# A searched schedule for a Sinkhorn attention and top-1 expert kernel

## Chip, core and metric

The kernel runs on one core of one Trainium2 chip, in a single launch. The metric is the device time of one execution in microseconds (us). The core has five engines that run side by side: TensorE (PE in the profile) multiplies matrices and writes to PSUM, a memory of eight banks; VectorE (DVE) and ScalarE (ACT) read PSUM and do the elementwise work; GpSimd (POOL) does elementwise work in SBUF, the core's main memory, and here issues the loads; SyncE (SP) issues the stores. An engine works off its instructions in the order in which the program emits them, so the order chosen at build time is what decides who waits.

## What is computed

Attention over blocks, with keys and values mixed between blocks by a matrix that five Sinkhorn rounds make from `sort_net`; then each of the 3072 tokens goes through one of eight experts, the one with the largest logit.

```python
batch, n_heads, seq, head_dim, n_blocks = 4, 8, 768, 64, 8        # float32 inputs

for _ in range(5):                                   # P = sort_net, one 8 x 8 matrix for each head
    P = P - np.max(P, axis=-1, keepdims=True)
    P = np.exp(P)
    P = P / (np.sum(P, axis=-1, keepdims=True) + 1e-09)
    P = P / (np.sum(P, axis=-2, keepdims=True) + 1e-09)
k_sorted = np.einsum('bhij,bhjcd->bhicd', P, k_b)    # v_sorted the same; k_b has 8 blocks of 96 rows
scores = scale * np.matmul(q_b, k_sb.transpose(0, 1, 2, 4, 3))      # each block with its mixed keys
attn = exp(scores - max) / (sum + 1e-09)
x = (attn @ v_sb)  as  [3072, 512]                   # heads side by side

logits = x @ w_gate                                  # [3072, 8]
expert_idx = np.argmax(logits, axis=1)
gate_w = softmax(logits)[chosen]
for e in range(8):
    h = np.maximum(x[mask] @ w1[e], 0.0)             # w1[e]: 512 x 1024
    out[mask] = gate_w[mask, None] * (h @ w2[e])     # w2[e]: 1024 x 512
```

## The kernel before

The four batches are worked off one after another, overlapped. For each batch the kernel guesses one expert from the mean of the values (a "vote"), loads that expert's weights only, and sends all the batch's tokens through it. Tokens that chose another expert get weight zero, and a general path at the end, behind an `If`, adds them; with this draw no token needs it, and its body isn't run.

The program is emitted by a planner that runs at build time. Every piece of work is a task with an engine (or a choice of two), a cost in us, the tasks that it comes after, and a priority. The planner simulates the engines, takes at each step the task that can start first (the lowest priority value among those within a short look ahead), and emits the instructions in this order. Where it foresees a gap on TensorE early on, it puts in idle matmuls.

```python
class Plan:
    LAG = {("pe", "act"): 0.3, ("pe", "dve"): 0.3, ("act", "pe"): 0.2, ...}
    FIRM, SWITCH, STAY = -900, 0.09, 20
    FETCH, QUIET = 6.0, (14.5, 17.0, 3.9)           # how soon TensorE's next 256 instructions are there

    def fill(self, t):
        at = self.free.get("pe", self.begin)
        while t.start < self.until and t.start - at > 0.25:
            n = 80 if at < self.warm else 512 if t.start - at > 0.5 else 128
            ...                                      # one idle matmul of n columns into a free bank
```

GpSimd issues the loads, which turn float32 into bfloat16 on the way. Their order is fixed by a chain:

```python
    def load_w1(ev, i, piece):                       # a quarter of the columns of all rows
        at = slice(piece * F // PIECES, (piece + 1) * F // PIECES)
        nc.gpsimd.dma_start(out=w1s[i][:, :, at], in_=w1_r[bass.ds(ev, 1), :, :, at].rearrange("e p c f -> p (e c) f"))

    def load_w2(ev, i, piece):
        at = slice(piece * FC // PIECES, (piece + 1) * FC // PIECES)
        nc.gpsimd.dma_start(out=w2s[i][:, at], in_=w2_r[bass.ds(ev, 1), :, at].rearrange("e p c d -> p (e c) d"))

    for name in ("zero vr1", "zero ksT1", "ones vs1", "rev", "ones", "expand k", "expand v"):
        later[name].behind = w2_at[0][-1]
    for b in range(2, B):
        later[f"vote add{b}"].behind = w2_at[b - 1][-1]

    chain = [*FIRST_LOADS, *loads(0)[2:], *w1_at[0], *w2_at[0], *loads(1)]
    chain += [later[n] for n in ("expand k", "expand v", "zero ksT1")] + loads(2)
    for b in range(1, B):
        chain += [*w1_at[b], *w2_at[b], *(loads(3) if b == 1 else [])]
```

Values are first laid out anew ("relay", into `vr`), on VectorE or, for batch 0, also on ScalarE. The vote of batches 1 to 3 adds up the 48 rows of each partition on GpSimd, by halves:

```python
            def run_add(e):
                tt = nc.gpsimd.tensor_add
                n = HB // 2
                tt(v_tmp, vr[i2][:, :, :n], vr[i2][:, :, n:HB])
                while n > 3:
                    n //= 2
                    tt(v_tmp[:, :, :n], v_tmp[:, :, :n], v_tmp[:, :, n:2 * n])
                tt(v_tmp[:, :, 0], v_tmp[:, :, 0], v_tmp[:, :, 1])
                tt(v_sum[i2].rearrange("p (d t) -> p d t", t=2), v_tmp[:, :, 0], v_tmp[:, :, 2])
```

Then follow: q transposed and k mixed (three groups each, evacuated from PSUM by ACT or DVE), v mixed (four groups), and eight steps of scores, exponential, product with v, normalising, transposing and copying to `xT`. The operands `expand_k` and `expand_v`, made on GpSimd, spread the Sinkhorn matrices of batches 1 to 3 over the partitions (`rep`, lines 516 and 542). The gate of a batch ends in `gws`:

```python
            nc.vector.scalar_tensor_tensor(out=gws[:, b], in0=picks[:, b, :, 0], scalar=top[b][:, :1],
                                           in1=gates[:, b], op0=ALU.is_equal, op1=ALU.mult)
```

The expert takes a batch in two halves of 384 tokens; the first half of batch 0 goes in two parts of 192:

```python
            parts = 2 if b == half == 0 else 1
            n = NH // parts
            for r, fc in ((r, fc) for r in range(parts) for fc in range(FC)):
                t = add(f"h{b}.{half}.{fc}.{r}", {"pe": 0.66 / parts + 0.02 * (parts - 1)}, ... mm_hidden(
                            bank(pb)[:, :n], w1s[i2], xTs[b], lo, lo + n, fc),
                        [w1_at[b][fc * PIECES // FC], *turn_of[b][s0:s0 + steps], *(hT_user[hi] or [])], at, opens=pb, n=DC)
                relus[r].append(add(f"relu{b}.{half}.{fc}.{r}", ...))
```

Of the kernel before, what the change touches and what calls it, by code (L numbers as in the profile page):

```python
# [13 lines left out]
ALU = mybir.AluOpType  # L14
# [15 lines left out]
class Banks:  # L30


    def __init__(self, n, only=None):
        self.n, self.only, self.at = n, only, None


class Plan:
# [9 lines left out]
    FETCH, QUIET = 6.0, (14.5, 17.0, 3.9)  # L47
    BLOCK_AT, BLOCK, PACE, WAIT = 191, 256, 12.5, 300

    def __init__(self, dma_at=2.1, begin=1.4, warm=5.6, until=32.0):  # L50
        self.begin, self.warm, self.until = begin, warm, until
        self.tasks, self.free = [], {}
        self.bank = [0.0] * 8
        self.dma_free = dma_at
        self.order = []
        self.mode = "full"
        self.count, self.block, self.fetched = 0, self.BLOCK_AT + self.BLOCK, None

# [26 lines left out]
    def due(self):  # L85

        return self.fetched + (self.QUIET[2] if self.QUIET[0] < self.fetched < self.QUIET[1] else self.FETCH)
# [16 lines left out]
    def fill(self, t):  # L104

        at = self.free.get("pe", self.begin)
        while t.start < self.until and t.start - at > 0.25:
            n = 80 if at < self.warm else 512 if t.start - at > 0.5 else 128
# [28 lines left out]

    def schedule(self):
        waiting = {t: len(t.after) for t in self.tasks}
# [7 lines left out]
        open_ = [t for t in self.tasks if not waiting[t]]  # L147
        seq = {t: i for i, t in enumerate(self.tasks)}
        firm = [t for t in self.tasks if t.prio < self.FIRM]
        while open_:  # L150
            choice = None
            soon, due = {}, []
            for t in firm:
                if t.start is not None:
                    continue
                at = 0.0
                for a in t.after:
                    e = next(iter(t.cost))
# [6 lines left out]
                if at is not None:  # L165
                    soon[t] = at + min(t.cost.values())
                    if len(t.cost) == 1:
                        due.append((next(iter(t.cost)), at))
            per = {}
            for t in open_:  # L170
# [6 lines left out]
                opts = []  # L177
                for e, us in t.cost.items():
                    if e == "pe" and t.mode != self.mode:
                        us += self.SWITCH  # L180
                    s = max(self.free.get(e, 0.0), bank_at)
                    for a in t.after:
                        lag = 0.0 if a.lands is not None else self.LAG.get((a.engine, e), 0.15)
                        s = max(s, a.end + lag)
                    if t.prio >= self.FIRM:
                        for d, at in sorted(due, key=lambda x: x[1]):
                            if d == e and s < at + 0.3 and s + us > at + 0.08:
                                s = at + 0.31
                    if e == "pe":
                        s = self.fetch(t, s, us)  # L190
                    opts.append((s + us, s, e))
                end, s, e = min(opts)
# [17 lines left out]
            if t.lands is not None:  # L210
                if t.lands:
                    rate = 2.43 if self.dma_free < 13 else 2.85
                    self.dma_free = max(self.dma_free, end + 0.9) + t.lands * rate
                    t.end = self.dma_free + 1.6
                else:
# [6 lines left out]
            if t.closes is not None:  # L222
                for i in range(t.closes.n):
                    self.bank[t.closes.at + i] = t.end
            self.order.append(t)
            open_.remove(t)
            for n in then[t]:
                waiting[n] -= 1
                if not waiting[n]:
                    open_.append(n)  # L230
# [6 lines left out]
def kernel(  # L237
# [67 lines left out]
    xTs = [sb([P, DC, S], BF16, f"xT{i}") for i in range(B)]  # L305
# [3 lines left out]
    outs = [sb([P, MD], F32, f"o{i}") for i in range(4)]  # L309
# [26 lines left out]

    engines = {"act": nc.scalar, "dve": nc.vector, "pool": nc.gpsimd}
# [20 lines left out]
    def add_load_q(b, after=()):  # L358
        q_at[b] = [add(f"load q{b}", {"pool": 0.73}, lambda e: load_qk(q, q_in, b, 0, CS),
                       after=[*after, *q_done.get(b - 2, [])], prio=b, lands=1.5)] * 3  # L360

    def add_load_k(b, parts, after=()):
        n = CS // parts
        got = []
        for i in range(parts):
            got.append(add(f"load k{b}.{i}", {"pool": 0.73},
                           lambda e, i=i: load_qk(k, k_in, b, i * n, n),
                           after=[*after, *k_done.get(b - 2, [])], prio=b, lands=1.5 / parts))
        k_at[b] = [got[g * parts // 3] for g in range(3)]

    def add_load_v(b, after=()):
        def run(e):
            nc.gpsimd.dma_start(out=v_in[b % 2], in_=v[b].rearrange("h (x c) d -> (h x) c d", c=HB))
        v_at[b] = add(f"load v{b}", {"pool": 0.73}, run,
# [8 lines left out]
    def load_w1(ev, i, piece):  # L383
        at = slice(piece * F // PIECES, (piece + 1) * F // PIECES)
        nc.gpsimd.dma_start(out=w1s[i][:, :, at], in_=w1_r[bass.ds(ev, 1), :, :, at].rearrange("e p c f -> p (e c) f"))  # L385
# [31 lines left out]
    for i in range(2):  # L417
# [6 lines left out]
        pads["vr", i] = add(f"zero vr{i}", {"pool" if i else "dve": 0.96 if i else 0.5}, zero_vr, prio=5 if i else -940)  # L424
        pads["ksT", i] = add(f"zero ksT{i}", {"pool": 1.9}, zero_ksT, prio=5 if i else FIRST + 7)
# [7 lines left out]
    for i in range(2):  # L433
        pads["vs", i] = add(f"ones vs{i}", {"pool": 1.0}, lambda e, i=i: ones_vs(e, i),
# [49 lines left out]
    ek1 = add("expand k", {"pool": 1.2}, lambda e: run_expand(expand_k, NB * CQ), [mk_ident], prio=5)  # L484
    ev1 = add("expand v", {"pool": 0.8}, lambda e: run_expand(expand_v, NB * 2), [mk_ident], prio=5)
# [123 lines left out]
    SPAN, PREP, STEPS, STEP = 100, 4, 40, 6.5  # L609
    RELAY = {"act": 0.86, "dve": 0.49}  # L610

    def add_attention(b):
# [5 lines left out]
        for d0 in range(0, D // 2, cut):  # L618
# [8 lines left out]
            relays.append(add(f"relay{b}.{d0}", {"dve": 0.82} if b else RELAY, run_relay,  # L627
# [13 lines left out]
        else:  # L641
            def run_add(e):
                tt = nc.gpsimd.tensor_add
                n = HB // 2
                tt(v_tmp, vr[i2][:, :, :n], vr[i2][:, :, n:HB])  # L645
                while n > 3:
                    n //= 2
                    tt(v_tmp[:, :, :n], v_tmp[:, :, :n], v_tmp[:, :, n:2 * n])  # L648
# [35 lines left out]
        w1_at[b] = [add(f"load w1.{b}.{r}", {"pool": 0.75 if r else 1.9}, lambda e, r=r: run_w1(e, r),  # L684
                        [t4, *relu_of.get(b - 2, [])], A - 20 if b else -940, lands=2.0 / PIECES)
                    for r in range(PIECES)]
        w2_at[b] = [add(f"load w2.{b}.{r}", {"pool": 0.65}, lambda e, r=r: load_w2(val["ev"], i2, r),
                        outs_of.get(b - 2, []), A - 20, lands=2.0 / PIECES) for r in range(PIECES)]
        top_at[b] = add(f"top{b}", {"pool": 0.2}, lambda e: nc.gpsimd.tensor_scalar(
# [28 lines left out]
        for g in range(3):  # L718
# [16 lines left out]
            def run_ev(e, g=g, kb=kb):  # L735
# [343 lines left out]
```

## Time and profile before

| what | value |
|---|---|
| time, median of 3 | 162.43 us (161.91 to 163.8) |
| profiled execution | 162.2 us, span 160.5 us |
| hidden matmuls (line 879) | 288, busy 49.9 us |
| output matmuls (line 884) | 200, busy 45.8 us |
| idle matmuls (line 120) | 98, busy 9.9 us |
| read from HBM, written to it | 35.68 MB, 6.29 MB |

The profile's views that matter here: the busy share of each engine, whole and in 40 slices of the span; the waits (who waited for whom: total us, times, longest); the chain of work that ended last, followed back from the end, as start, length and what ran; and the timeline, all instructions in order of time with the idle time ahead of each. "L879" is line 879 of the kernel. PEld is the loading of weights into TensorE. A busy TensorE includes time in which matmuls only overlap in its pipeline, so the length of a chain piece divided by its matmuls tells more than the mean of one. PEclk is the clock that TensorE was granted, in tenths.

### The profile page before, as it was taken

The page shows a single profiled execution, that of the slowest core. Times are in us where ns is not written, and L with a number is a line of the kernel's source. Part 1 is how long each engine was busy: PE and PEld are TensorE (multiplying, and loading weights), DVE is VectorE, ACT ScalarE, POOL GpSimd, SP SyncE. Part 2 cuts the span into 40 slices and gives each one's busy share as a digit, 9 for nine tenths or more (in the row PEclk, how much of TensorE's full clock was granted, in tenths as well). Part 3 has the DMA queues.
Part 4 walks back from the last instruction along what each step waited for, and adds up shares of the span by engine and source line. Part 5 has one row for each costly group of instructions (what it writes and reads, how often), then busy time and mean ns, then how long its engine had stood idle before and what let it go on. Part 6 is the DMA issues. An engine that isn't in the chain of part 4 may idle for free.

```text
span 160.5 us, 5478 instructions
## 1 busy us (share of the span) xinstructions
PE 146.1 (91%) x2313; PEld 98.1 (61%) x2313; DVE 87.4 (54%) x220; ACT 97.2 (61%) x163; POOL 66.4 (41%) x110
## 2 busy tenths in 40 slices
PE   6989888699899999779999999999999999999950
PEld 6758767595656656537556666675566656545440
DVE  4885788669938928712946674383446734400010
ACT  3159897373777596624567867576578465637340
POOL 6940795996920968929379100950000000000000
PEclk9999999999999999987999999999999999999999
DMA  3999499999999999999999902799831023023051
GB/s 20 193 202 185 52 141 202 216 211 213 222 230 253 222 197 232 250 233 212 204 197 245 230 10 69 116 217 201 173 114 44 0 69 131 0 77 124 0 178 32
DMA packets 20301, 24.55 MB, mean 153 GB/s; under 512 B 1712, under 2 KB 15024, under 8 KB 20272
## 3 DMA queue, kind: packets, MB, share of 16 engines
q0 software_dynamic: 16096, 17.83, 67.0%
q1 hardware_dynamic: 4032, 6.19, 11.2%
q8 instruction: 20, 0.33, 0.8%
q10 hardware_dynamic: 144, 0.13, 0.2%
q14 instruction: 9, 0.07, 0.1%
HBM read 35.68 MB, written 6.29 MB: 261 GB/s over the span
## 4 chain that ended last, share of the span: by engine, by line
PE 73%; DMA 8%; POOL 6%; DVE 6%; issue 3%; ACT 1%; DVEq 0%; POOLq 0%
PE psum L879 27%; PE psum L884 24%; DMA k_in<-in_k_dram 8%; PE psum L802 4%; PE psum L821 4%; PE psum L786 4%; PE psum L725 3%; PE psum L702 3%; PE psum L753 3%; POOL v_tmp L645 2%; POOL v_tmp L648 2%; DVE gws L870 2%; PE psum L846 2%; ACT ex L795 1%; DVE vr L626 1%
## 5 line engine op out<-in xcount | busy, mean ns | idle before, releaser
L879 PE MATMUL psum<-xT,w 128*128 128x384 bf16 (+1 forms) x288 | 49.9, 315 | 0.0
L884 PE MATMUL psum<-w,hT 128*128 128x512 bf16 (+1 forms) x200 | 45.8, 371 | 0.1
L889 ACT ACTIVATE hT<-psum 128x384 bf16<-128x384 f32 (+1 forms) x61 | 27.9, 461 | 17.1 <-PE psum L879 16.6
L879 PEld LDWEIGHTS <-w 128*128 128x128 bf16 x288 | 25.3, 99 | 12.3 <-issue 1.2
L884 PEld LDWEIGHTS <-hT 128*128 128x128 bf16 x200 | 17.9, 98 | 17.3
L795 ACT ACTIVATE ex<-psum 128x768 bf16<-128x768 f32 x32 | 24.1, 813 | 2.4 <-PE psum L786 1.5
L385 POOL DMA_DIRECT2D w<-in_moe_w_dram x16 | 12.1, 772 | 28.2 <-issue 16.9
L813 DVE TENSOR_TENSOR xo<-psum,rec 96x512 bf16<-96x512 f32 x32 | 22.0, 687 | 1.2 <-DVE rec L812 0.2
L895 ACT ACTIVATE o<-psum,gws 128x512 f32<-128x512 f32 (+1 forms) x18 | 12.2, 676 | 16.8 <-PE psum L884 14.9
L897 DVE TENSOR_SCALAR o<-psum,gws 128x512 f32<-128x512 f32 (+1 forms) x7 | 4.9, 711 | 20.9 <-PE psum L884 20.6
L341 ACT CAST vs<-psum 128x1024 bf16<-128x1024 f32 x12 | 12.1, 1018 | 4.1 <-PE psum L753 3.7
L802 PEld LDWEIGHTS <-ex 128*128 128x128 bf16 x256 | 10.8, 97 | 3.7 <-ACT ex L795 0.4
L389 POOL DMA_DIRECT2D w<-in_moe_w_dram x16 | 11.4, 744 | 3.3 <-PE psum L884 2.9
L802 PE MATMUL psum<-vs,ex 128*128 128x65 bf16 x256 | 12.2, 193 | 0.3 <-ACT ex L795 0.3
L343 DVE COPY xT<-psum 128x384 bf16<-128x384 bf16 x23 | 8.2, 354 | 7.6 <-PE psum L821 7.2
L821 PE MATMUL psum<-ident,xo 96*128 96x96 bf16 x128 | 10.9, 206 | 0.6 <-issue 0.6
L120 PE MATMUL psum<-idle 128*128 128x80 bf16 (+2 forms) x98 | 9.9, 280 | 1.3 <-DVE idle L426 1.3
L821 PEld LDWEIGHTS <-xo 96*128 96x128 bf16 x128 | 8.1, 97 | 4.7 <-issue 0.7
L753 PE MATMUL psum<-pv,vr 128*64 128x64 bf16 x512 | 10.2, 197 | 0.4 <-issue 0.4
L753 PEld LDWEIGHTS <-vr 128*64 128x64 bf16 x512 | 9.1, 112 | 2.1 <-issue 1.5
L812 DVE RECIPROCAL rec<-psum 96x8 f32<-96x8 f32 x32 | 6.3, 198 | 7.3 <-PE psum L802 7.3
L645 POOL TENSOR_TENSOR v_tmp<-vr 128x1536 bf16<-128x1536 bf16 x3 | 9.3, 3096 | 1.7 <-DVE vr L626 1.5
(105 smaller groups left out, 169.3 us busy)
## 6 DMA issues: line engine op xcount, KB each, us to landing
w<-in_moe_w_dram POOLq DMA_DIRECT2D x32, 256.0 KB, 9.1
out_dram<-o SPq DMA_DIRECT2D x23, 256.0 KB, 4.0
q_in<-in_q_dram POOLq DMA_DIRECT2D x4, 768.0 KB, 16.3
v_in<-in_v_dram POOLq DMA_DIRECT2D x4, 768.0 KB, 13.6
k_in<-in_k_dram POOLq DMA_DIRECT2D x3, 768.0 KB, 19.1
k_in<-in_k_dram POOLq DMA_DIRECT2D x3, 256.0 KB, 11.7
out_dram<-o ACTq DMA_DIRECT2D x1, 128.0 KB, 3.6
out_dram<-o SPq DMA_DIRECT2D x1, 128.0 KB, 3.0
```

The costliest lines, as they stand in the source:

```text
L341: nc.scalar.copy(dst, src)
L385: nc.gpsimd.dma_start(out=w1s[i][:, :, at], in_=w1_r[bass.ds(ev, 1), :, :, at].rearrange("e p c f -> p (e c) f"))
L645: tt(v_tmp, vr[i2][:, :, :n], vr[i2][:, :, n:HB])
L753: nc.tensor.matmul(out=t[f * HP:(f + 1) * HP, u, :], lhsT=vr[i2][:, d // 2, :, d % 2], rhs=pv[b][:, f * H:(f + 1) * H, :].rearrange("p h i ...
L795: te = add(f"exp{b}.{i}", {"act": 0.82}, lambda e, ex=ex, sbk=sbk: nc.scalar.activation(ex[:, :H * BLK].rearrange("p (t c) -> p t c", t=2) ...
L802: nc.tensor.matmul(out=av[:, h // 4, h % 4, :], lhsT=ex[:, h * BLK:h * BLK + P], rhs=vs[i2][:, h * NB + i, :D + 1], start=(h % 4 == 0), st ...
L813: nc.vector.tensor_mul(xo, av[:, :, :, :D], rec.to_broadcast([BLK, 2, 4, D]))
L821: nc.tensor.transpose(out=tp[:, dc, :], in_=xf[:, dc * P:(dc + 1) * P], identity=ident[:BLK, :BLK])
L879: nc.tensor.matmul(out=ps, lhsT=w1t[:, dc, fc * P:(fc + 1) * P], rhs=xT[:, dc, lo:hi], start=(dc == 0), stop=(dc == DC - 1))
L884: nc.tensor.matmul(out=ps, lhsT=hT[:, fc, s * P:(s + 1) * P], rhs=w2t[:, fc, d0:d1], start=(fc == 0), stop=(fc == FC - 1))
L889: nc.scalar.activation(dst, src, ACT.Relu)
L895: nc.scalar.activation(dst, src, ACT.Copy, scale=gw)
```

## The change

The planner gets a better model of the chip and a search; some work moves between engines and in time.

- **Search.** The planner schedules 1500 times with priorities shifted at random, singly, in small groups or for all tasks of a kind, and keeps a shift if the planned end isn't later.
- **Model.** Costs and landings of GpSimd's loads and operations are reset, at most eight loads are taken to be outstanding on its queue, the time to TensorE's next 256 instructions depends on the time in the kernel, and idle matmuls go only into gaps over 0.5 us.
- **GpSimd.** `zero vr1`, `zero ksT1`, `expand k` and `expand v` are made ahead of the first weights and not after them. The first addition of a vote is cut into four, the next into two. GpSimd does one of the four relays of batch 0.
- **Weights.** w1 comes in quarters of its rows (whole rows of 1024) and not of its columns; the hidden matmuls then wait for all four quarters.
- **Relus.** In the parts of 192 tokens, two hidden blocks share a PSUM bank and one relu.
- **Last k group of batch 0.** Its evacuation is split between ACT and DVE.
- **Stores.** The first five output tiles are stored in two pieces each.
- **General path.** It becomes a short loop in a loop; `xT` and the output buffers become one tile each for it.

```diff
-    FETCH, QUIET = 6.0, (14.5, 17.0, 3.9)
+    FETCH = ((14.0, 6.0), (17.0, 3.9), (33.0, 6.8), (118.0, 6.0), (999.0, 4.0))
+    RING = 8
-        while t.start < self.until and t.start - at > 0.25:
-            n = 80 if at < self.warm else 512 if t.start - at > 0.5 else 128
+        while t.start < self.until and t.start - at > 0.5:
+            n = 80 if at < self.warm else 512
+    def search(self, rounds, seed, width=20.0, calm=-900):
+        rng = random.Random(seed)
+        best = self.schedule()
+        some = [t for t in self.tasks if t.prio >= calm]
+        ...
+        for _ in range(rounds):
+            if rng.random() < 0.3:
+                group = rng.choice(kinds)
+                shift = rng.gauss(0.0, width)
+                moved = [(t, t.prio, shift) for t in group]
+            else:
+                group = rng.sample(some, rng.choice((1, 1, 2, 4, 8)))
+                moved = [(t, t.prio, rng.gauss(0.0, width)) for t in group]
+            ...
+            end = self.schedule()
+            if end <= best:
+                best = end
+            else: ...                                # the old priorities again
+                    elif e == "pool" and t.lands:
+                        s = max(s, self.ring[-self.RING])
...
-                       after=[*after, *q_done.get(b - 2, [])], prio=b, lands=1.5)] * 3
+                       after=[*after, *q_done.get(b - 2, [])], prio=b, lands=1.5 if b else 1.7)] * 3
-                           after=[*after, *k_done.get(b - 2, [])], prio=b, lands=1.5 / parts))
+                           after=[*after, *k_done.get(b - 2, [])], prio=b, lands=1.5 / parts + (0.4 if b == i == 0 else 0.0)))
...
-        at = slice(piece * F // PIECES, (piece + 1) * F // PIECES)
-        nc.gpsimd.dma_start(out=w1s[i][:, :, at], in_=w1_r[bass.ds(ev, 1), :, :, at].rearrange("e p c f -> p (e c) f"))
+        at = slice(piece * DC // PIECES, (piece + 1) * DC // PIECES)
+        nc.gpsimd.dma_start(out=w1s[i][:, at], in_=w1_r[bass.ds(ev, 1), :, at].rearrange("e p c f -> p (e c) f"))
...
-        pads["ksT", i] = add(f"zero ksT{i}", {"pool": 1.9}, zero_ksT, prio=5 if i else FIRST + 7)
+        pads["ksT", i] = add(f"zero ksT{i}", {"pool": 0.96}, zero_ksT, prio=FIRST + 9 if i else FIRST + 7)
-    ek1 = add("expand k", {"pool": 1.2}, lambda e: run_expand(expand_k, NB * CQ), [mk_ident], prio=5)
-    ev1 = add("expand v", {"pool": 0.8}, lambda e: run_expand(expand_v, NB * 2), [mk_ident], prio=5)
+    ek1 = add("expand k", {"pool": 0.82}, lambda e: run_expand(expand_k, NB * CQ), [mk_ident], prio=FIRST + 10)
+    ev1 = add("expand v", {"pool": 0.5}, lambda e: run_expand(expand_v, NB * 2), [mk_ident], prio=FIRST + 10)
...
+    RELAY_ON = {0: {"dve": 0.49}, 8: {"act": 0.86}, 16: {"pool": 0.86}, 24: {"dve": 0.49}}
-            relays.append(add(f"relay{b}.{d0}", {"dve": 0.82} if b else RELAY, run_relay,
+            relays.append(add(f"relay{b}.{d0}", {"dve": 0.82} if b else RELAY_ON[d0], run_relay,
...
-                tt(v_tmp, vr[i2][:, :, :n], vr[i2][:, :, n:HB])
+                cuts = 4
+                for i in range(cuts):
+                    at = slice(i * D // 2 // cuts, (i + 1) * D // 2 // cuts)
+                    tt(v_tmp[:, at], vr[i2][:, at, :n], vr[i2][:, at, n:HB])
                 while n > 3:
                     n //= 2
-                    tt(v_tmp[:, :, :n], v_tmp[:, :, :n], v_tmp[:, :, n:2 * n])
+                    cuts = max(cuts // 2, 1)
+                    for i in range(cuts):
+                        at = slice(i * D // 2 // cuts, (i + 1) * D // 2 // cuts)
+                        tt(v_tmp[:, at, :n], v_tmp[:, at, :n], v_tmp[:, at, n:2 * n])
...
+            if b == 0 and g == 2:
+                for lo, e in ((0, "act"), (1, "dve")):
+                    k_ev.append(add(f"k ev{b}.{g}.{lo}", {"act": {"act": 0.62}, "dve": {"dve": 0.69}}[e],
+                                    lambda e, run_ev=run_ev, lo=lo: run_ev(e, lo=lo, hi=lo + 1), [t], LAST_K, closes=kb))
...
-            for r, fc in ((r, fc) for r in range(parts) for fc in range(FC)):
+            group = min(512 // n, 4)
+            for r, fc in ((r, fc) for r in range(parts) for fc in range(0, FC, group)):
...
-                        [w1_at[b][fc * PIECES // FC], *turn_of[b][s0:s0 + steps], *(hT_user[hi] or [])], at, opens=pb, n=DC)
+                        [*w1_at[b], *turn_of[b][s0:s0 + steps], *(hT_user[hi] or [])],
+                        at, opens=pb, n=group * DC)
...
-    for name in ("zero vr1", "zero ksT1", "ones vs1", "rev", "ones", "expand k", "expand v"):
+    for name in ("ones vs1", "rev", "ones"):
         later[name].behind = w2_at[0][-1]
-    chain += [later[n] for n in ("expand k", "expand v", "zero ksT1")] + loads(2)
+    chain += loads(2)
...
-    plan.schedule()
+    plan.search(rounds=1500, seed=4)
```

## The prediction

> **What bounds the kernel now.** I read the busy-time part of the page first, then the waits of TensorE, then the chain of waits, then the timeline around the waits. The first lines:
>
> ```profile
> PE 146.1 (91%) x2313; PEld 98.1 (61%) x2313; DVE 87.4 (54%) x220; ACT 97.2 (61%) x163; POOL 66.4 (41%) x110
> ...
> POOL 6940795996920968929379100950000000000000
> PEclk9999999999999999987999999999999999999999
> DMA  3999499999999999999999902799831023023051
> ```
>
> TensorE is busy 91% of the span; no other engine passes 61%. Columns of the last three rows are slices of 4.0 us. The 16 DMA engines are full from about slice 6 to slice 22, yet that alone does not say that anyone waits for them. TensorE's own list of waits between 17 and 75 us, whole:
>
> ```profile
> PE psum L655 <- POOL v_sum L650: 2.2, 1, 2.2
> PE psum L516 <- DVE xo L813: 1.4, 1, 1.4
> PE psum L702 <- DVE o L897: 0.8, 1, 0.8
> PE psum L821 <- issue: 0.6, 1, 0.6
> PE psum L786 <- ACT ex L795: 0.6, 1, 0.6
> PE psum L753 <- issue: 0.4, 1, 0.4
> PE psum L802 <- ACT ex L795: 0.3, 1, 0.3
> ```
>
> These add up to 6.3 us, and none is a DMA. From 75 to 155 us the same view is empty, and the table of busy time by stage has TensorE at 64.00 of 64.00 us from 75 to 139. So the end is a fixed amount of matmul work laid behind whatever was lost before 75 us: **each us of TensorE idleness removed before 75 us ends the kernel one us earlier**, and nothing done after it helps unless it takes matmul work away. After the last matmul (154.9) there is a tail of 5.6 us (last weighing, store, closing barrier) to the span's end at 160.5. The timed 162.43 us is 1.9 above the span.
>
> Three of the waits have a visible cause. The chain of waits, start and length in us:
>
> ```profile
> 28.68 0.69 DVE xo L813
> 29.37 0.13 DVE rec L812
> 29.52 0.70 DVE xo L813
> 30.23 0.34 PE psum L516 x6
> ...
> 38.70 2.84 DVE gws L870
> 41.63 0.76 DVE o L897
> 42.44 0.64 PE psum L702 x16
> ...
> 62.23 3.11 POOL v_tmp L645
> 65.40 1.65 POOL v_tmp L648
> ...
> 69.40 0.19 PE psum L655
> 69.60 0.76 PE psum L879 x4
> 70.35 0.28 PE psum L665 x8
> 70.64 3.60 PE psum L879 x12
> ```
>
> First, L516 multiplies by expand_k. The chain names DVE, but the timeline has expand_k's copy on GpSimd starting at 29.36 and lasting 0.81, so it ends at 30.17, just ahead of the weight load at 30.22. TensorE stood 1.41 us before that. Second, gws has 6 elements per partition and takes 0.22 to 0.23 us in three batches, but 2.83 in batch 0, where it lies exactly beside the first vote add (38.41, 3.10 us). It held the weighing that emptied the PSUM bank that TensorE wanted: 0.76 us lost. Third, the vote of batch 2: its additions start at 62.23 because GpSimd's queue has eleven load issues ahead of them, and the matmul that needs the sum stands 2.21 us. Behind it 12 matmuls of 384 columns take 3.60 us, 0.30 each, where the pieces of 8 at 90.1 and 91.6 us take 1.30 (0.163 each), at which 12 would need 1.96. So 1.64 us go on a halved clock (the 8 and 7 in the clock row). The third wait costs 2.21 + 1.64 = **3.85 us**.
>
> **What the Trainium skill says.** "SBUF — State Buffer", Who interferes with whom: a VectorE operation with two SBUF inputs is blocked by a GpSimd operation that reads SBUF for as long as that operation lasts. The trace agrees: gws 2.83 us beside a 3.10 us addition, 0.23 otherwise. "TensorE: Matmul & The Clock Gate", Part 1 (The HAM clock gate): after an idle window of about 3.4 us TensorE runs at half clock. The trace shows the half clock after a wait of only 2.21 us, and it lasts about as long as those 12 matmuls, 3.6 us. "DMA: Bandwidth & Descriptors", Why small descriptors are slow: a packet carries a fixed cost, so larger ones move more. In the table of queues 15,024 of 20,301 packets are under 2 KB; w1 is among the small ones, as a quarter of its columns is 256 elements, 512 B as bf16.
>
> **The change, part by part.**
>
> (a) GpSimd operands ahead of the weights. expand_k, expand_v, the zeros of vr1 and ksT1 (0.81 + 0.50 + 0.95 + 0.94 = 3.2 us) move from 28.5 to 31.5 us into GpSimd's hole of 7.24 us ahead of the first w1 load (17.10). They fit beside the relay that GpSimd newly takes (about 0.86 by the change's own cost). The 1.41 us wait loses its cause, and the loads of batch 2, issued at 31.46 behind them, come 3 us sooner. I count -1.2, as some of the gap is also DVE's.
>
> (b) The vote additions cut in 4, 2, 1, 1. A piece of the first is about 3.10 / 4 plus a fixed part: from 1536, 768, 384, 192 elements in 3.10, 1.64, 0.90, 0.51 us I get 1.9 ns per element and about 0.15 us fixed, so 0.9 us a piece. gws can then be held 0.9 and not 2.8 us: saving up to 1.9 on DVE, and the whole 0.76 on TensorE; I count -0.6. Four extra operations add 4 x 0.15 = 0.6 us on GpSimd, to its 7.1 per vote.
>
> (c) The planner knows the limit of eight outstanding loads on GpSimd's queue (RING), better costs of its operations and later landings (k's first piece, q0), and searches 1500 times over priorities for an earlier end. The 3.85 us exist because the plan put the vote's matmul where it thought the sum was ready. If the new plan knows when GpSimd gets there, it places other matmuls ahead. I give this three chances in four: -2.9.
>
> (d) The last k evacuation of batch 0 is split over ACT and DVE. Now DVE works off two in 2.57 us, until 19.06, and the first score matmul starts at 19.24, 1.5 us after the last k matmul (17.72). Two halves by the change's costs (0.62 and 0.69) would be done near 18.5. The fourth relay going to GpSimd frees 0.85 us of ACT at 14.18. I count -0.6; the rest meets ACT, whose exponentials (0.81 each, eight) pace this stretch.
>
> (e) Fills only for gaps over 0.5 us: six of 128 columns at 22.4 and 23.6 cost 0.17 + 0.27 in the chain; -0.3.
>
> (f) Paired relus in the first half: 16 of 192 columns (0.34 us) become 8 of 384 (0.49): 16 x 0.34 - 8 x 0.49 = 1.5 us off ACT and DVE, which at 28 to 32 us are busy only 1.29 and 2.71 of 4. Worth 0 on the path.
>
> (g) w1 by rows: 2 KB packets in place of 512 B, so the weights land sooner as a whole, but no hidden matmul starts before all four pieces are there. The first now starts at 24.33, with w1 issued from 17.10 to 20.09. A landing takes 9.1 us in the middle, so a later start is possible: +0.3.
>
> (h) Search on the rest: 0.6 + 0.6 + 0.4 + 0.3 us of small waits; I count -0.7. A different plan meets chip waits that it does not know: +1.3. The general path as loops isn't run (no matmul of it is in the trace); TensorE's long branch at the end is hidden behind the last store: 0. Two stores per early tile only add SP issues: 0.
>
> Sum: -1.2 - 0.6 - 2.9 - 0.6 - 0.3 + 0.3 - 0.7 + 1.3 = **-4.7**, so 162.4 - 4.7 = 157.7. I say **157.5 us**, 3% faster.
>
> **Rivals.** (1) The plan is only as good as its model. A search drives the plan into corners of it: 1500 tries take out slack that the chip needs, and new stalls of 2 us with a halved clock behind them come back. For it: the 3.85 us stall is exactly such a miss of the old model. Against: the changed constants move towards this trace (q0 used at 8.87, v0 at 12.5). It would leave 160 to 163. (2) The weights become the bound in batch 0: all of w1, then w2, must land, and DMA is full from 24 us on. If the first hidden matmul slips from 24.3 to 27, the attention of batch 0 alone can't fill TensorE, and 1.5 to 2.5 us of the gain go: about 159.5. For it: the four pieces are now needed together. Against: the larger packets. (3) ACT and DVE pace batch 0 whatever the order: eight steps of exponential, reciprocal, normalising and copy are about 0.81 + 0.20 + 0.69 + 0.36 = 2.06 us on two engines, 8.2 us for the batch, while TensorE has some 5.1 us of attention work there (0.24 + 0.23 + 0.17 a step in the chain). Then (d) and (h) bring nothing: 159. (4) The search fills all known holes: removing 6.3 + 1.6 + 0.4 us of loss, and the start being 0.6 sooner, gives 153.5.
>
> **Range and chances.** Rival 4 sets the low side, 153.5; rival 1 the high side, 161.5. A 2% gain needs 159.2: all of (a) to (h) but 1.5 us may fail, or the second vote's stall alone together with (a) must survive. Faster by over 2%: 0.70; within: 0.24; slower: 0.06, since the matmul work is the same and something must be newly lost to be slower.
>
> **What would show it.** Right: no wait of TensorE for v_sum and a clock row of nines until the tail; expand_k before the first w1 issue and L516's successor with no wait; gws of batch 0 under 1.2 us; TensorE gapless from some time before 70 us; the last matmul near 150. Matmul counts of the hidden and output lines unchanged (288 and 200), idle matmuls fewer than 98. Wrong: TensorE waiting for w or for ACT near 24 us, a new clock dip, or matmul time in the steady stretch that differs from 0.163 us per 384 columns, as then the work itself has changed and not its gaps.

## The result and the profile after

The changed kernel takes 155.46 us in the median (154.08 to 155.65), where the kernel before takes 162.29 beside it: a ratio of 0.955, with a 95% interval of 0.948 to 0.963. That is 6.8 us less. The predicted 157.5 us was 2.0 us too high; its terms summed to -4.7.

The profiled execution took 154.08 us with a span of 152.5 us. Its page has these lines for the busy time and for the slices (3.8 us each; the rows are GpSimd's busy tenths, TensorE's clock and the DMA's share, and the last line counts packets):

```profile
PE 143.1 (94%) x2292; PEld 96.9 (63%) x2292; DVE 85.8 (56%) x216; ACT 96.4 (63%) x159; POOL 67.6 (44%) x123
...
POOL 6997698459954839938209921920000000000000
PEclk9999699999999999999999999999999999999998
DMA  2999499999999999999999983899612020112134
...
DMA packets 14235, 24.52 MB, mean 161 GB/s; under 512 B 1792, under 2 KB 6912, under 8 KB 14208
```

The 8 and 7 in the middle of the clock row are gone. A 6 early in the row is new. Nearly all bytes are as before (24.52 MB for 24.55) in 30% fewer packets (14,235 for 20,301). TensorE's waits between 17 and 155 us, whole (who waited for whom: total us, times, longest):

```profile
PE psum L870 <- ACT ex L879: 0.7, 2, 0.4
PE psum L870 <- DVE ksT L413: 0.4, 1, 0.4
PE psum L962 <- DMA w<-in_moe_w_dram: 0.4, 1, 0.4
```

1.5 us of waiting remain of 6.3, all of it before 26 us, and none is for the vote's sum. The chain of waits of this profile holds one piece only, so where the three old causes went has to be read from the timeline. GpSimd from 11 us (start, length, engine and line, operation, and in brackets the idle time ahead of it):

```profile
11.92 0.81 POOL L552 COPY expand_k<-ident 32x768 bf16<-32x768 bf16 x1
12.69 0.50 POOL L552 COPY expand_v<-ident 32x384 bf16<-32x384 bf16 x1
13.14 1.13 POOL L698 COPY vr<-v_in 128x384 uint32<-128x384 uint32 x1
16.52 2.29 POOL L455 DMA_DIRECT2D w<-in_moe_w_dram  x4 [2.25 <-issue]
```

The operands now stand before the first weights, as the prediction asked. VectorE in batch 0's gate, beside the cut addition:

```profile
36.87 0.74 DVE L944 SCALAR_TENSOR_TENSOR key<-sh,rev 128x48 f32<-128x48 f32 x1
...
38.22 0.23 DVE L953 SCALAR_TENSOR_TENSOR gws<-picks,top,gates 128x6 f32<-128x6 f32 x1
```

`gws` takes 0.23 us for 2.83 before; only `key` is held a little (0.74). And GpSimd at the second vote, which is where the two kernels differ most:

```profile
48.36 2.31 POOL L455 DMA_DIRECT2D w<-in_moe_w_dram  x4 [0.51 <-issue]
50.73 2.12 POOL L459 DMA_DIRECT2D w<-in_moe_w_dram  x3
55.67 0.71 POOL L459 DMA_DIRECT2D w<-in_moe_w_dram  x1 [2.82 <-DVE xo L897]
56.41 3.52 POOL L720 TENSOR_TENSOR v_tmp<-vr 128x384 bf16<-128x384 bf16 x4
59.90 3.33 POOL L726 TENSOR_TENSOR v_tmp<-v_tmp 128x384 bf16<-128x384 bf16 x4
...
63.68 0.29 POOL L728 TENSOR_TENSOR v_sum<-v_tmp 128x64 bf16<-128x64 bf16 x1
63.92 0.58 POOL L443 DMA_DIRECT2D v_in<-in_v_dram  x1
64.50 0.71 POOL L426 DMA_DIRECT2D q_in<-in_q_dram  x1
65.19 0.72 POOL L426 DMA_DIRECT2D k_in<-in_k_dram  x1
```

The same stretch in the kernel before:

```profile
55.06 2.85 POOL L389 DMA_DIRECT2D w<-in_moe_w_dram  x4
58.32 0.55 POOL L373 DMA_DIRECT2D v_in<-in_v_dram  x1 [0.41 <-DMA w<-in_moe_w_dram]
59.87 0.70 POOL L356 DMA_DIRECT2D q_in<-in_q_dram  x1 [1.00 <-PE psum L802]
61.17 0.71 POOL L356 DMA_DIRECT2D k_in<-in_k_dram  x1 [0.60 <-PE psum L884]
...
62.23 3.10 POOL L645 TENSOR_TENSOR v_tmp<-vr 128x1536 bf16<-128x1536 bf16 x1
```

Before, the additions started at 62.23, behind eight weight loads and the three loads of batch 3, and ended at 69.35. Now the three loads stand behind the additions, which start at 56.41 and end at 63.97. TensorE's matmul on the sum runs at 64.23 without a wait. The last matmul ends at 147.98 (154.81 before). The part from there to the end of the span is 4.6 us, where it was 5.7.

The two spans differ by 8.0 us, and the traces say where: 5.2 us up to the matmul on the second vote's sum (64.23 for 69.40), 1.7 from there to the last matmul (83.75 us long for 85.41, about the 1.64 that the prediction had put down to the half clock), 1.1 after it.

### The profile page after: what moved, and what is told of

It reads as the page before. It is cut to its first block, busy times and chain, and to the rows that moved or that the text cites. A ratio compares the mean times of both kernels' runs of the same rounds, so it can differ in the third digit from the quotient of the medians.

```text
span 152.5 us, 5450 instructions
## 1 busy us (share of the span) xinstructions
PE 143.1 (94%) x2292; PEld 96.9 (63%) x2292; DVE 85.8 (56%) x216; ACT 96.4 (63%) x159; POOL 67.6 (44%) x123
## 2 busy tenths in 40 slices
DMA packets 14235, 24.52 MB, mean 161 GB/s; under 512 B 1792, under 2 KB 6912, under 8 KB 14208
## 5 line engine op out<-in xcount | busy, mean ns | idle before, releaser
L962 PE MATMUL psum<-xT,w 128*128 128x384 bf16 (+1 forms) x288 | 48.1, 308 | 0.4 <-DMA w<-in_moe_w_dram 0.4
L972 ACT ACTIVATE hT<-psum 128x384 bf16<-128x384 f32 x56 | 27.5, 491 | 17.1 <-PE psum L962 17.0
L978 ACT ACTIVATE o<-psum,gws 128x512 f32<-128x512 f32 (+1 forms) x20 | 13.6, 678 | 15.0 <-PE psum L967 14.1
L459 POOL DMA_DIRECT2D w<-in_moe_w_dram x16 | 11.5, 720 | 10.0 <-DVE rec L896 3.8
L980 DVE TENSOR_SCALAR o<-psum,gws 128x512 f32<-128x512 f32 (+1 forms) x5 | 3.5, 697 | 16.8 <-PE psum L967 15.4
L413 DVE CAST vs<-psum 128x1024 bf16<-128x1024 f32 x8 | 9.7, 1221 | 4.4 <-PE psum L837 4.0
L455 POOL DMA_DIRECT2D w<-in_moe_w_dram x16 | 8.8, 548 | 7.2 <-issue 2.8
L837 PE MATMUL psum<-pv,vr 128*64 128x64 bf16 x512 | 10.9, 201 | 0.0
L837 PEld LDWEIGHTS <-vr 128*64 128x64 bf16 x512 | 10.0, 117 | 1.4 <-issue 1.4
L720 POOL TENSOR_TENSOR v_tmp<-vr 128x384 bf16<-128x384 bf16 x12 | 10.6, 910 | 0.0
L411 ACT COPY qT<-psum 128x1024 bf16<-128x1024 bf16 x10 | 9.7, 1017 | 1.3 <-PE psum L780 1.2
```

The source lines that it names most:

```text
L413: engines[e].tensor_copy(dst, src)
L720: tt(v_tmp[:, at], vr[i2][:, at, :n], vr[i2][:, at, n:HB])
L837: nc.tensor.matmul(out=t[f * HP:(f + 1) * HP, u, :], lhsT=vr[i2][:, d // 2, :, d % 2], rhs=pv[b][:, f * H:(f + 1) * H, :].rearrange("p h i ...
L962: nc.tensor.matmul(out=ps, lhsT=w1t[:, dc, fc * P:(fc + 1) * P], rhs=x[:, dc], start=(dc == 0), stop=(dc == DC - 1))
L972: nc.scalar.activation(dst, src, ACT.Relu)
L978: nc.scalar.activation(dst, src, ACT.Copy, scale=gw)
```

## Experiments

The theory, formed from these traces: **the order of GpSimd's queue** at the second vote gives most of the gain, since loads that must stand until earlier ones have landed no longer block the additions. Rivals: the early operands and the cut additions (terms (a) and (b)), the search itself, and larger packets. Six kernels take the changed kernel apart, four build it up from the one before, and two ask about its start. Where an edit names `plan.order`, all other tasks keep their places. Times from here on are medians without the executions that took over 1.5% longer than the fastest one of their kernel, each set beside the kernel before on the same chip, and the ratios have their 95% interval in brackets.

### Operands early, in the kernel before

```diff
+    early = [later[n] for n in ("zero vr1", "zero ksT1", "expand k", "expand v")]
+    kept = [t for t in plan.order if t not in early]
+    at = kept.index(w1_at[0][0])
+    plan.order = kept[:at] + early + kept[at:]
     order = ExitStack()
```

> The kernel before in its own order, with the four GpSimd operands (expand_k, expand_v, the zeros of vr1 and ksT1) moved ahead of the first w1 load. Theory K (knock-on: each stall before 75 us delays the votes and so feeds the stall of the second vote): TensorE's wait of 1.4 us ahead of expand_k's matmuls goes, the GpSimd loads that follow come about 3 us sooner, and the wait for the second vote's sum shrinks from 2.2 us to under 1 without a halved clock: 157.5 to 159.5. Theory M (the vote's stall is a miss of the plan by itself, whatever came before): only the 1.4 us go, 160.5 to 161.5. Rival: some of the gap was DVE's, 161.5 to 162.3.

Measured: 161.91 us beside 162.26 for the kernel before, ratio 0.997 (0.9945 to 1.0004). The profiled execution took 163.36 us, but its clock row has nines up to the second vote. The wait of `L516` is gone, and TensorE's two longest waits are now:

```profile
PE psum L655 <- POOL v_sum L650: 3.2, 1, 3.2
PE psum L702 <- DVE o L897: 1.5, 1, 1.5
```

They were 2.2 and 0.8. In this profile the vote's additions still start at 61.85 (62.23 before). TensorE came earlier to a sum that came when it always had. **The 1.4 us saved were handed to the next wait.** Term (a) alone is worth nothing measurable here, and Theory K, by which the wait for the sum would shrink, is refuted.

### Operands early and additions cut

To the edit above, the change's own `run_add` (4, 2, 1, 1 pieces).

```diff
-                tt(v_tmp, vr[i2][:, :, :n], vr[i2][:, :, n:HB])
+                cuts = 4
+                for i in range(cuts): ...            # as in the change
```

> The kernel before in its own order, operands early and the vote additions cut as in the change. The gate of batch 0 is then held at most about 0.9 us and not 2.8: against the run with the operands early alone, 0.3 to 0.8 us less; the second vote's sum comes about 0.5 us later by the extra pieces. Theory K: 157 to 159, with no halved clock in the middle. Theory M: 160 to 161, the stall of the second vote still above 2 us.

Measured: 164.09 us, ratio 1.013 (1.0095 to 1.0163), so it is 1.3% slower. `gws` is down to 0.43 us at most, and yet:

```profile
PE psum L661 <- POOL v_sum L656: 5.8, 1, 5.8
```

```profile
56.92 0.71 POOL L389 DMA_DIRECT2D w<-in_moe_w_dram  x1 [2.08 <-DMA k_in<-in_k_dram]
58.31 0.54 POOL L373 DMA_DIRECT2D v_in<-in_v_dram  x1 [0.68 <-DMA w<-in_moe_w_dram]
59.93 0.70 POOL L356 DMA_DIRECT2D q_in<-in_q_dram  x1 [1.07 <-PE psum L827]
61.98 0.71 POOL L356 DMA_DIRECT2D k_in<-in_k_dram  x1 [1.35 <-PE psum L885]
...
63.04 3.52 POOL L648 TENSOR_TENSOR v_tmp<-vr 128x384 bf16<-128x384 bf16 x4
```

In the brackets is the cause. The eighth weight load and each load of batch 3 stand 0.7 to 2.1 us before they can be issued. Twice the profile names the landing of an earlier load, twice a TensorE piece that these loads do not use. The landing times settle it: each of the four issues begins 0.28 to 0.55 us after an earlier load landed, and each time seven others are still under way, issued and not yet landed. The three loads of the kernel before follow landings in the same way (58.02, 59.32 and 60.64 us), and in none of the fourteen traces does GpSimd issue a load with more than seven earlier ones under way. The additions behind them do not start sooner whatever TensorE does, and cut they take longer (7.55 us for 7.12). Half clock lasts from 67.3 to 74.1 us, half of it within the wait and half behind it. Neither theory had foreseen a growing stall.

### Vote ahead of the loads, in the kernel before

```diff
+    three = loads(3)                                 # v, q and k of batch 3
+    kept = [t for t in plan.order if t not in three]
+    at = kept.index(later["vote add2"]) + 1
+    plan.order = kept[:at] + three + kept[at:]
     order = ExitStack()
```

> The kernel before in its own order, except that GpSimd issues the three loads of batch 3 after the vote additions of batch 2 and not ahead of them. Theory Q (the second vote is late because these loads stand in GpSimd's queue until earlier loads land): the additions start near 58 and not at 62.2, the sum is there near 65, before TensorE reaches it (67.2), the wait of 2.2 us and the half clock (1.6) go: 158 to 159. Rival C (the vote is late because everything before it is late): the additions hardly start sooner, 161.5 to 162.3. Rival D (batch 3's loads, issued 7 us later, are then missed): some other wait for loads, 160 to 162.

Measured: 157.95 us beside 161.27, ratio 0.983 (0.975 to 0.991), or -3.3 us (between 1.4 and 4.0 by the interval) from moving three instructions on one queue. The profiled execution took 160.63 us, 2.7 above the median, so only its order and its list of waits are read:

```profile
60.04 3.09 POOL L645 TENSOR_TENSOR v_tmp<-vr 128x1536 bf16<-128x1536 bf16 x1
...
66.86 0.29 POOL L650 TENSOR_TENSOR v_sum<-v_tmp 128x64 bf16<-128x64 bf16 x1
67.09 0.62 POOL L373 DMA_DIRECT2D v_in<-in_v_dram  x1
```

No wait for `v_sum` is left; those for `L516` (1.4) and for `o` (0.8) are as before.

### All three moves, in the kernel before

The three edits above together.

```diff
+    three = loads(3)                                 # behind "vote add2"
+    early = [...]                                    # ahead of the first w1 load
+                cuts = 4                             # in run_add
```

> The kernel before in its own order with three moves: the loads of batch 3 behind the vote additions of batch 2, the four GpSimd operands ahead of the first w1 load, the additions cut. Theory Q: with GpSimd no longer held up, what the two other moves save reaches the end, 156 to 157.5, thus most of the whole change without any search. Rival C: about as the operands early and cut alone, 163 to 164.

Measured: 156.80 us, ratio 0.974 (0.967 to 0.982). On top of the moved loads, the early operands and the cut additions bring 157.95 - 156.80 = 1.2 us. They were worth nothing without it. TensorE waits 0.7 us for `v_sum` and 0.6 at most for anything else; the part behind the last matmul is still 5.7 us. So 4.5 us (156.80 for 161.27) come without any search and without the new estimates, about two thirds of the gain.

### The reverse: loads ahead of the vote, in the changed kernel

The edit of the last but one, without `+ 1`.

```diff
+    at = kept.index(later["vote add2"])
+    plan.order = kept[:at] + three + kept[at:]
```

> The changed kernel in its own order, except that GpSimd issues the three loads of batch 3 ahead of the vote additions of batch 2, as in the kernel before. Theory Q: the additions start near 61 and not at 56.4, TensorE (there at 64.2 now) waits 3 to 5 us for the sum and then runs at half clock for a while: 159 to 161. Rival C: the other changes carry it, 155 to 156.5.

Measured: 159.19 us, ratio 0.987 (0.983 to 0.991), which is 3.7 us above the changed kernel's first median and 5.4 above its second (153.83, below, on another chip). Its longest wait, and GpSimd around it:

```profile
PE psum L733 <- POOL v_sum L728: 2.8, 1, 2.8
```

```profile
56.81 0.54 POOL L443 DMA_DIRECT2D v_in<-in_v_dram  x1 [0.55 <-DMA w<-in_moe_w_dram]
58.36 0.70 POOL L426 DMA_DIRECT2D q_in<-in_q_dram  x1 [1.01 <-PE psum L905]
59.60 0.71 POOL L426 DMA_DIRECT2D k_in<-in_k_dram  x1 [0.53 <-PE psum L967]
60.33 3.52 POOL L720 TENSOR_TENSOR v_tmp<-vr 128x384 bf16<-128x384 bf16 x4
```

The additions start at 60.33, where they started at 56.41, and a wait of 2.8 us returns with some 3.4 us of half clock behind it. Both directions agree: the place of these three loads is worth some 3 us in the kernel before and 4 to 5 in the changed one, half to two thirds of the gain.

### No search

```diff
-    plan.search(rounds=1500, seed=4)
+    plan.schedule()
```

> The changed kernel with its first plan in place of the best of 1500. The plan itself ends 2.4 us later than the searched one (156.1 against 153.7 by its own reckoning). If the gain is from the truer model and the moved work (theory T): 157.0 to 158.5, thus most of the 7 us stay. If it is from the search (theory S): 160 to 162.

Measured: 154.98 us, ratio 0.957 (0.953 to 0.961). That lies between the changed kernel's two medians, 155.46 and 153.83, so the search is not shown to bring anything; by the second median it would be 1.1 us. The planned ends are 155.0 for the kernel before, by its own older estimates, 156.1 without and 153.7 with search. On the chip the kernel before is the slowest of the three by far, and the 2.4 us that the search gains in the plan are not seen. The additions of the second vote start at 56.86 here too, ahead of the three loads.

### Search with the old estimates

All of the change, but the planner's figures as before: no limit on outstanding loads, old costs of GpSimd's operations, old landings, old times to the next instructions.

```diff
-    FETCH = ((14.0, 6.0), (17.0, 3.9), (33.0, 6.8), (118.0, 6.0), (999.0, 4.0))
-    RING = 8
+    FETCH = ((14.5, 6.0), (17.0, 3.9), (999.0, 6.0))
+    RING = 999
     ...                                              # costs and landings as before
```

> The changed kernel with the search, planned with the estimates of before (landings, costs on GpSimd, no limit of eight loads, the old fetch times). Its plan ends 1.5 us later by its own, more hopeful reckoning (155.3). Theory T (a truer model matters): the chip falls behind the plan as it did before, stalls of 1 to 2 us return, 157.5 to 160. Theory S (the search matters, the estimates little): 155 to 156.5.

Measured: 159.32 us, ratio 0.982 (0.979 to 0.986). The three longest waits:

```profile
PE psum L886 <- ACT ex L879: 1.9, 2, 1.4
PE psum L803 <- DMA k_in<-in_k_dram: 1.8, 1, 1.8
PE psum L733 <- POOL v_sum L728: 1.3, 2, 0.9
```

The three loads stand ahead of the vote again (57.11 to 60.07, additions from 60.80), and the clock halves twice, from about 17.6 to 21 and from 24.4 to 31 us. **Searching on the old estimates gives up 4 to 5 us; the new ones without a search lose 1 us at most by the medians.** Which of the old figures costs how much is not separated here, though the limit of eight loads is the one that knows of the queue. Each search was run with one seed only, so how much of its result is chance is open.

### Additions in one piece

```diff
-                cuts = 4
+                cuts = 1
```

> The changed kernel in its own order, the vote additions uncut. Theory G (a long addition holds the gate of batch 0): the gate takes up to 3 us again in place of 0.23, and the first weighing and what needs its bank come later: 0.3 to 1 us more than the changed kernel. Rival: the new order has nothing that waits for it, and the additions are 0.6 us shorter a vote: the same or 0.3 us less.

Measured: 157.47 us beside 153.83 for the changed kernel on the same chip, so +3.6; ratio to the kernel before 0.973 (0.969 to 0.977). The timeline of all engines:

```profile
36.83 3.10 POOL L720 TENSOR_TENSOR v_tmp<-vr 128x1536 bf16<-128x1536 bf16 x1 [1.54 <-DVE vr L698]
...
37.22 2.77 DVE L944 SCALAR_TENSOR_TENSOR key<-sh,rev 128x48 f32<-128x48 f32 x1
...
40.60 1.06 DVE L953 SCALAR_TENSOR_TENSOR gws<-picks,top,gates 128x6 f32<-128x6 f32 x1
...
41.69 0.69 ACT L978 ACTIVATE o<-psum,gws 128x512 f32<-128x512 f32 x1 [3.39 <-DVE gws L953]
...
42.43 1.44 PE L962 MATMUL psum<-xT,w 128*128 128x384 bf16 x4 [2.58 <-ACT o L978]
```

Read from the bottom: TensorE stands 2.58 us for a PSUM bank that ScalarE empties with `gws`, which is late because `key` lay beside the uncut addition until 39.99 and `gws` (1.06 us for 0.23) beside the next one. This agrees with what the Trainium skill says in "SBUF — State Buffer", Who interferes with whom, and shows its price here: 2.6 us, and from 41.9 to 45.3 us the half clock. This execution took 158.82 us, the longest of the six, so the half clock may not be part of the median's +3.6.

### The old general path

The changed kernel with the unrolled general path of the kernel before (not run with this draw in either).

```diff
-    with tc.If(rv > 0):                              # short loop in a loop
+    with tc.If(rv > 0):                              # unrolled, as in the kernel before
```

> The changed kernel with the general path of before (batches and halves written out inside the loop over experts; not run with this data). Theory L (jumping over the long body costs time at the end): TensorE's branch takes about 4 us again and not 0.2, and the closing part from the last matmul to the end of the span grows from 4.5 to 5 to 5.6 us: 156 to 157. Rival: the last store hides it, 155 to 155.8.

Measured: 155.88 us (154.85 to 156.81), ratio 0.967 (0.960 to 0.974). By the times alone this can't be told from the changed kernel. The profiles show the mechanism: TensorE's branch over the body (min, median and max in ns, then the start in us), first with the old path, then in the changed kernel:

```profile
L1122 PEldq COMPARE_BRANCH  x1: 4272/4272/4272, 146.2 to 146.2; - x1
```

```profile
L1122 PEldq COMPARE_BRANCH  x1: 223/223/223, 145.4 to 145.4; - x1
```

In the kernel before it took 4.02 us. The part from the last matmul to the end of the span is 6.4 us with the old path, 4.6 in both profiles of the changed kernel, 5.7 in the kernel before. The Trainium skill's "Runtime: NRT & Kernel Launch", Instruction fetch mechanics, says that a taken branch beyond the instructions at hand has to fetch its target first; the two durations fit that. By these profiles 1.1 to 1.8 us come from it. Among all fourteen profiles the closing part is 5.3 to 6.4 us with the long body (six) and 3.3 to 5.0 with the short one (eight), so the direction is clear; as the times overlap, the size is not settled.

### w1 by columns

```diff
-        at = slice(piece * DC // PIECES, (piece + 1) * DC // PIECES)
+        at = slice(piece * F // PIECES, (piece + 1) * F // PIECES)     # columns; all four are waited for
```

> The changed kernel in its own order, w1 loaded in quarters of its columns as before (512 B pieces), all four still waited for. Theory P (small packets are slower): packets rise from 14,235 to about 20,300, TensorE's wait for w near 25.8 us grows from 0.4 to 1.5 to 2.5 us, 0.8 to 2 us more than the changed kernel. Rival: the DMA engines are no bound of the time, within 0.3 us of it.

Measured: 155.40 us beside 153.83, so +1.6; ratio 0.960 (0.956 to 0.965), against 0.950 (0.946 to 0.955) for the changed kernel on the same chip. The intervals only just part. The wait for w does not grow: it is 0.2 us. What comes later is the value load of batch 1, here and then in the changed kernel's first profile, which has the same clock dip at the start:

```profile
35.85 1.58 DVE L698 COPY vr<-v_in 128x768 uint32<-128x768 uint32 x2 [1.92 <-DMA v_in<-in_v_dram]
```

```profile
34.58 1.82 DVE L698 COPY vr<-v_in 128x768 uint32<-128x768 uint32 x2 [0.77 <-DMA v_in<-in_v_dram]
```

1.27 us later, and TensorE then waits 0.5 us for `vr`. So by this comparison larger packets help, through the load queued behind w1 and not through w1. As the changed kernel's first median, 155.46, is no lower than 155.40, the size is not settled.

### The changed kernel again, and with a warmer start

The first was run unchanged. The second adds six idle matmuls of 512 columns to the gaps of the first 18 us, to keep the clock up.

```diff
+    for name, more in (("pt first0", 4), ("vote pick0", 1), ("k0.0", 1)):
+        later[name].spares += later[name].spares[-1:] * more
```

> The changed kernel itself, once more, on the same chip and beside the same runs of before as the next three. All theories: 154.5 to 156. It is the measure for them; its closing part (last matmul to the end of the span) is to be compared with that of the run with the old general path.

> The changed kernel in its own order with six more idle matmuls of 512 columns in gaps between 10 and 15 us (four ahead of the first Sinkhorn product, one ahead of the vote's pick, one ahead of the first k group), about as many as the kernel before has there. Theory W (the half clock from 14.5 to 17.9 us delays the first scores): no half clock before 20 us, the first score matmul near 18.7 and not 19.9, 0.5 to 1.3 us less than the changed kernel: 154 to 155. Rival (w1, landed near 25.5, and ACT's exponentials set the pace of this stretch): the scores start sooner, the hidden matmuls don't, 155 to 155.6.

Measured: 153.83 us (153.65 to 154.09) and 154.25 (153.88 to 154.65); ratios 0.950 (0.946 to 0.955) and 0.953 (0.949 to 0.957). The 6 in the clock row of the first profile is a dip from 14.5 to 17.9 us. One slice of the busy time by stage (window, length, then PE, PEld, DVE, ACT, POOL busy with their counts, clock, DMA share, GB/s), in the first profile of the changed kernel and in its second:

```profile
16.00:17.00 1.00, 1.00 (x40) 1.00 (x38) 0.00 (x0) 0.79 (x1) 0.48 (x1) 0.50 0.05 8
```

```profile
16.00:17.00 1.00, 1.00 (x60) 1.00 (x52) 0.79 (x1) 1.00 (x2) 0.47 (x1) 1.00 0.14 28
```

At half clock the first score matmul starts at 19.93 us, without the dip at 18.87, yet the two spans are 152.5 and 152.2: 1.1 us early on is worth 0.3 at the end. Part of the reason shows in the waits. With the dip TensorE waits 0.4 us for w at 25 us, without it 0.6, with the warm start 0.8: 0.2 to 0.4 us of what the start wins is spent on weights that have not landed. The warm start has no lower median; its 154.25 us lies in the range of Theory W only because the unchanged kernel came out below what was expected of it. That the six matmuls remove the dip is not shown by the profiles, as the unchanged kernel's second one lacks it too. The granted clock over the whole execution is 0.994 or more in five of six executions with them and in two of eleven without, so they seem to make it rarer.

## Why the prediction came out as it did

It named the right places, and 155.46 us lies in its range. Its largest term has nearly the right size for a reason that failed, which is luck, and other terms were off in both directions.

- **(c) The second vote, -2.9: the place is right, the reason is not.** The step that failed is "it places other matmuls ahead". In both traces 104 hidden and 48 output matmuls stand ahead of the one on the sum. TensorE does not come to it later but 3 us sooner (at 64.23 us, where it began to wait at 67.2); the sum itself comes 5.4 us sooner (63.97 for 69.35). Of this 3.9 come from the three loads behind the additions (additions at 56.41, at 60.33 with the loads back in front). Alone this move is -3.3 us, near the 2.9 that was counted for other reasons. I had read "eleven load issues ahead of them" and taken it for a queue that is only long. The brackets in front of its last three issues (0.41, 1.00 and 0.60 us) would have said that it stands.
- **(a) Operands, -1.2, and (b) cut, -0.6: right in sum, wrong as separate terms.** Alone (a) is 0 and (a) with (b) costs 1.3% of the time, as long as the vote has its own fixed time; behind (c) the two bring 1.2 us of the 1.8. So the step "each us of TensorE idleness removed before 75 us ends the kernel one us earlier" failed as well: the 1.4 us of (a) went into the next waits (1.0 us more for the sum, 0.7 for `o`). In the changed order the cut is worth 3.6 us, because there TensorE stands 2.58 us. **A term read from one trace held only for that trace's order.**
- **(h) Search, -0.7 and +1.3: a gain by the search is not shown.** Without it the time lies between the two medians of the changed kernel. 1.5 us of waits remain, most of them new ones.
- **(g) w1 by rows, +0.3: the wait is right (0.4 us), the sign of the term is not.** By columns costs about 1.6 us in the one comparison that was made, through a load that I did not look at.
- **(d) k evacuation, -0.6, and (e) fills, -0.3.** The first score matmul starts at 18.87 for 19.24 where the clock is full, so -0.4; at half clock 19.93. The prediction had named a new clock dip as a sign of being wrong, and one came, in a place where 1.1 us costs only 0.3. Whether the fewer fills cause it was not tried by themselves.
- **The general path, 0: wrong.** "TensorE's long branch at the end is hidden behind the last store" does not hold: with the short body the branch takes 0.22 us for 4.0 and the closing part shrinks from 5.7 to 4.6 us.
- **(f) Paired relus, 0**, were not tried alone; no wait of the new profile points to them.

The parts that were measured going up from the kernel before are 3.3 us for the loads and 1.2 for operands and cut, and the closing part is 1.1 shorter by the profiles: 5.6 of the 6.8 us. The rest is not attributed; rows of w1 may bring something, and the early clock dip takes something back.

Of the rivals, (1) did not come true with the new estimates; under the old ones the searched plan does meet new stalls (1.4 and 1.8 us the longest) and takes 159.3 us, so the rival is right for a search on an untrue model. (2) and (3) show only as the 0.4 and 0.7 us of waits that remain for w and for ScalarE. (4) asked for all holes filled at 153.5, and the changed kernel's second median of 153.83 comes close: not all holes are filled, but the closing part also shrank, which it did not count. No version that was run clearly beats the changed kernel.

## What to carry over

On an engine that issues loads and also computes, read the idle time in front of each issue: a load that has to stand until earlier ones have landed blocks every computation behind it, and moving it behind them cost nothing here, where its data was not needed soon. A single saving in front of a wait with a time of its own is swallowed by it, so look for the wait that ends last before adding up terms. Here truer estimates were worth 4 to 5 us to the scheduler and 1500 tries about 1 at most by the medians; which of the estimates did it was not tried.

## What the runs showed of the hardware that was not expected

- In none of the fourteen traces is a load issued from GpSimd while more than seven earlier ones are under way. Issues that had to stand for this began 0.28 to 0.61 us after an earlier load landed.
- TensorE waits of 2.2 us (kernel before), 2.58 (additions in one piece) and 2.8 (loads ahead of the vote) each came with some 3.4 us of half clock, which began 2.1 to 3.8 us after the wait did. A wait of 5.8 us came with some 6.7, beginning 2.5 us after its start.
- Not only `gws` but also `key`, with 48 elements and normally about 0.2 us, is held for 2.77 us by an addition of 3.10 us; beside pieces of 0.9 us it takes 0.59 and 0.74 in two profiles of the changed kernel.
- A TensorE branch over a long body takes 4.0 to 4.3 us, over a short one 0.22 to 0.24; VectorE's and SyncE's take 0.05 to 0.07 in either case.
- Issuing a quarter of w1 costs GpSimd about 0.55 us by rows and 0.77 by columns.
